# Sliding-window attention beside a gated layer: logits, softmax and weights of two chunks in one group each

## The chip, the cores and the metric

The kernel runs on one core of one Trainium2 chip. The metric is the device time of one execution in microseconds (us); the kernel before takes 259.79 us, the median of three runs (259.69 to 259.99). The engines that matter: TensorE (PE in the profile, PEld for its weight loads), VectorE (DVE), ScalarE (ACT), GpSimd (POOL) and SyncE (SP), which here issues most transfers.

## The reference

One input x (`A_x`, 2048 tokens by 640 features) goes through a layer norm. The normed x feeds two branches, an attention over a short dilated window and a gated layer, and both are added to x. The input `B_x` is not used.

```python
def _A_ref(x, wqkv, wo):            # 32 heads of 20, window W = 8, dilation 2
    qkv = ((x @ wqkv).reshape(B, S, 3, H, Dh)).transpose(2, 0, 3, 1, 4)
    q, k, v = qkv[0], qkv[1], qkv[2]
    idx = pos[:, None] - off[None, :]          # pos - 0, 2, 4, ... 14
    kg, vg = k at idx, v at idx                # (B, H, S, W, Dh)
    logits = einsum("bhsd,bhswd->bhsw", q, kg) * Dh ** -0.5
    logits = where(idx >= 0, logits, -1e9)
    o = einsum("bhsw,bhswd->bhsd", softmax(logits), vg)
    return o.transpose(0, 2, 1, 3).reshape(B, S, D) @ wo

def _B_ref(x, w_gate, w_up, w_down):           # 640 -> 1536 -> 640
    return ((x @ w_gate) * (x @ w_up)) @ w_down

xn = layernorm(A_x)
out = A_x + _A_ref(xn, A_wqkv, A_wo) + _B_ref(xn, B_w_gate, B_w_up, B_w_down)
```

## The kernel before

The 2048 tokens are four chunks (`NCH`) of 512 (`CS`), each four token tiles of 128 (`CH` = 4, `P` = 128). Features lie on the 128 partitions, 640 of them in five slices (`KT`). Head h owns four partitions (`JL`) of every slice, so a sum over a head's features is a sum over five slices and four partitions.

The stages of a chunk c:

- **Projections** (`proj`, L487 to L505): q, k and v, each five groups of five matmuls of 512 columns into PSUM tiles `ps` (six banks in turn), copied to SBUF by ScalarE (L498).
- **Products** (`products`, L543 to L563): for each half chunk of 256 tokens (`HS`), eight offsets in four VectorE multiplications q times shifted k into two tiles `pw` (L557), then **folds** (`fold`, L522): three additions each that sum the five slices; the last (L533) writes into the places of k and q that are no longer needed.
- **Logits** (`logits`, L569): matmuls with `Ek`, a matrix of 128 by 32 that sums each head's four partitions. Tokens of a half chunk are cut in four parts of 64 (`E` = HS // 4), and part j goes to the array's column strip j and thus to partitions 32j to 32j+31. So a group n = 2c + g is a PSUM tile `lps` of 128 partitions (part and head) by 8 offsets by 64 tokens: 512 floats, one PSUM bank, tag `pl` with two buffers. It is eight matmuls of 256 columns (L579), two groups per chunk.
- **Softmax** (`softmax`, L595): per group, on that tile in place: maximum over the offsets (L607), subtraction (L611), Exp on ScalarE (L620), sum (L627), reciprocal (L630), product into `a` (L634). Group 0 adds the mask first (L603).
- **Weights**: `store` (L640) writes `a` to a DRAM scratch tile `aD`, 128 KB, and `spread` (L646) reads it back into `aE` with each head's weights repeated on its four partitions, 512 KB, two buffers. Both are issued by SP.
- **Values** (`av`, L661): per token tile two multiplications of v by `aE`, one for each part of 64 tokens, 2560 elements each (L674); three additions that sum the eight offsets (L684 twice, L682) end in `oT`.
- **Gated layer** (`glu`, L708): twelve times five matmuls each for gate and up (L717), copies by ScalarE (L722), their product `hT` on VectorE (L734).
- **Output** (`down`, L769): per token tile and half of the 640 outputs, twelve matmuls from `hT` (L783) and five from `oT` (L786) add up in one PSUM bank; ScalarE copies them out (L798), and GpSimd adds them to the output in DRAM. For the first tile of a chunk the matmuls of `hT` 10 and 11 come last. The last two tiles go through VectorE (L794).

Nothing is written in the order in which it runs. Each step is registered by `add` with an engine, a planned cost, the part of it that occupies the engine (`occ`), and its dependencies; `Plan.order` then lists them. At each turn it takes the engine that is free first and, among its steps that are ready, the one that must be done first (`late`, counted back from the end); on TensorE all steps but the logits are a fixed chain (`main`), and logits are `urgent`: they go in as soon as the plan has them ready. `margin` adds time after a step's inputs before the plan takes it to be ready: 0.9 us for logits of chunk 0 and 2 for the others. `PACE` multiplies all planned times of an engine: 1.03 for VectorE. Engines then run their own lists in that order, and a step that isn't ready holds up what stands behind it.

```python
    PACE = {"DVE": 1.03, "ACT": 1.0}
```
```python
        LL[n].margin = (0.9 if c == 0 else 2) if alone else 0.0
```

The names in dependencies: `PW` products, `FO` folds, `LL` logits, `AA` the finished weights in SBUF, `AS` the store, `AE` the spread, `AM` a tile's last multiplication, `O16` and `OE` its oT, `HT` hT, `DT` a tile's last matmul. A spread waits for `AM.get(2 * n - 3)`, the last tile of the group two before. The first multiplication of a tile follows `AM.get(t - 1)`, since `ONE` is False.

The main loop at the end takes attention, gated layer, layer norm of chunk c + 2, output and the projections of chunk c + 2 for each c; the projections of chunks 0 and 1 come ahead.

Of the kernel before, what the change touches and what calls it, by code (L numbers as in the profile page):

```python
# [10 lines left out]
ALU = mybir.AluOpType  # L11
# [21 lines left out]
class Plan:  # L33
# [1 line left out]

    LAG = 0.06
    RAW = 0.116
    PACE = {"DVE": 1.03, "ACT": 1.0}
    INORDER = ("DVE", "PE", "ACT")

    def __init__(self):
# [70 lines left out]
def kernel(  # L112
# [314 lines left out]
            X[t + 5] = add("POOL", 6.0, load_x(t + 5, nc.gpsimd), [a], occ=0.45, kb=160)  # L427

    LL = {}
    PV = {}  # L430
    R = {}
    PROJ = ("q", "k", "v")
# [2 lines left out]
    def halo(c, r):  # L435
        def fn():
            k = new((PROJ[r], c), [P, KT, HALO + CS], BF, PROJ[r], 2)
            if c == 0:
                nc.gpsimd.memset(k[:, :, 0:HALO], 0.0)
            else:  # L440
                nc.scalar.copy(k[:, :, 0:HALO], T[PROJ[r], c - 1][:, :, CS : CS + HALO])
        if c == 0:
            HALOCP[r, c] = add("POOL", 0.3, fn, after=[RS[0]])
        else:
            w = LL.get(2 * c - 3) if r == 1 else O16.get(CH * (c - 1) - 1)
            HALOCP[r, c] = add("ACT", 0.25, fn, [w, *R[r, c - 1]])

    def lhs(r, i, j):
# [38 lines left out]
    def proj(c, r, lo=0, n=CS):  # L487
        for j in range(KT):
            key = ("qkv", c, r, j, lo)

            def pe(key=key, j=j):
                new(key, [P, 512], F32, "ps", 6, psum)
                for i in range(KT):
                    nc.tensor.matmul(T[key][:, 0:n], lhsT=lhs(r, i, j),  # L494
                                     rhs=T["xnT", c][:, i, lo : lo + n], start=(i == 0), stop=(i == KT - 1))

            def ev(key=key, j=j):
                nc.scalar.copy(where(r, c, j, j + 1, lo, n)[:, 0, :], T[key][:, 0:n])  # L498

            ts = range(c * CH + lo // P, c * CH + (lo + n) // P)  # L500
            old = LL.get(2 * c - 3) if r < 2 else O16.get(CH * (c - 1) - 1)
            a = pe_main(KT * (n / 2400 + 0.0027), pe, [*WW[r], *[TT[t] for t in ts], *[TX.get(t) for t in ts], old])
            e = add("ACT", 0.16 + n / 1200, ev, [a, HALOCP.get((r, c)), R.get((r, c - 2), [None])[0]], occ=0.07 + n / 1200)
            ring.append(e)
            R.setdefault((r, c), []).append(e)  # L505
# [37 lines left out]
    def products(c, hf):  # L543
        for j in range(4):
            i = 4 * hf + j
            u = i // 2

            def mul(u=u, j=j):
                if j % 2 == 0:
                    new(("pw", c, u), [P, 4, KT, HS], BF, *(("av", 2) if c == 0 and hf else ("pw", 2)))  # L550
                o = T["pw", c, u][:, 2 * (j % 2) : 2 * (j % 2) + 2, :, :]
                lo = hf * HS
                qh = T["q", c][:, :, lo : lo + HS]
                kh = T["k", c][:, :, lo + DIL * 2 * j : lo + DIL * 2 * j + HS]
                qh = bass.AP(tensor=qh.tensor, offset=qh.offset, ap=[list(qh.ap[0]), [0, 2], *[list(x) for x in qh.ap[1:]]])
                kh = bass.AP(tensor=kh.tensor, offset=kh.offset, ap=[list(kh.ap[0]), [DIL, 2], *[list(x) for x in kh.ap[1:]]])
                nc.vector.tensor_tensor(o, qh, kh, ALU.mult)  # L557

            m = 8 * c + i
            w = None if c == 0 else LL[0] if c == 1 and hf == 0 and FIRST < 3 else FO[4 * c + u - 2]  # L560
            PW[m] = add("DVE", 1.48, mul, [*R[0, c], *R[1, c], w], occ=1.395, after=[PW.get(m - 1)])
        for u in (2 * hf, 2 * hf + 1):
            FO[4 * c + u] = fold(c, u)  # L563

    PAIRED = ()

    E = HS // 4

    def logits(c, g):  # L569
        n = 2 * c + g  # L570

        def lg():
            l = new(("lps", n), [P, W, E], F32, "pl", 2, psum)
            parts = [summed(c, 2 * g + b) for b in range(2)]
            last = len(parts[0]) - 1
            for i in range(last + 1):
                for b in range(2):
                    for j in range(4):
                        nc.tensor.matmul(l[H * j : H * (j + 1), 4 * b : 4 * b + 4, :], lhsT=Ek[:],  # L579
                                         rhs=parts[b][i][:, :, E * j : E * (j + 1)],  # L580
                                         start=(i == 0 and b == 0), stop=(i == last), tile_position=(0, H * j), skip_group_check=True)

        alone = not (g and c in PAIRED)
        took = 0.022 + 0.2195 * (len(LEFT) if c == 0 else 1) + (0.19 if alone else 0.0)
        LL[n] = add("PE", took + 0.13, lg, [FO[2 * n], FO[2 * n + 1], FO[4 * c + 3] if c in PAIRED else None, LL.get(n - 1), AA.get(n - 2), CE], occ=took)
        LL[n].urgent = True
        LL[n].margin = (0.9 if c == 0 else 2) if alone else 0.0

    def prodlog(c):
        for g in range(2):  # L590
            products(c, g)
        for g in range(2):
            logits(c, g)

    def softmax(c, hf):  # L595
        n = 2 * c + hf

        def small(op, occ, deps):
            return add("DVE", occ + 0.083, op, deps, occ=occ)

        def mask():
            ps = T["lps", n]
            nc.vector.tensor_tensor(ps[0:H, :, 0:HALO], ps[0:H, :, 0:HALO], negm[0:H], ALU.add)  # L603

        def top():
            m = new(("m", n), [P, E], F32, "m", 1)
            nc.vector.tensor_reduce(m[:], T["lps", n][:].rearrange("p w s -> p s w"), AX.X, ALU.max)  # L607

        def sub():
            d = T["d", n] = T["lps", n]  # L610
            nc.vector.tensor_tensor(d[:], d[:], T["m", n][:, None, :].to_broadcast([P, W, E]), ALU.subtract)  # L611

        a = LL[n]
        if n == 0:
            a = small(mask, 0.18, [a, CM])
        a = small(top, 0.6, [a])
        DD[n] = small(sub, 0.609, [a, AA.get(n - 1)])

        def ex():
            nc.scalar.activation(T["d", n][:], T["d", n][:], ACT.Exp, scale=scale)  # L620

        e = add("ACT", 0.635, ex, [DD[n]], occ=0.54)
        e.margin = 0.8

        def total():
            s = new(("s", n), [P, E], F32, "s", 1)
            nc.vector.tensor_reduce(s[:], T["d", n][:].rearrange("p w s -> p s w"), AX.X, ALU.add)  # L627

        def rec():
            nc.vector.reciprocal(T["s", n][:], T["s", n][:])  # L630

        def scaled():
            a = new(("a", n), [P, W, E], BF, "a", 1)
            nc.vector.tensor_tensor(a[:], T["d", n][:], T["s", n][:, None, :].to_broadcast([P, W, E]), ALU.mult)  # L634

        AA[n] = small(scaled, 0.609, [small(rec, 0.47, [small(total, 0.6, [e])]), AS.get(n - 1)])

        def store():
            aD = new(("aD", n), [H, 4, W * E], BF, "aD", 2, dram)
            nc.sync.dma_start(out=aD[:].rearrange("h e f -> e h f"), in_=T["a", n][:].rearrange("p w s -> p (w s)"))  # L640

        def spread():
            ae = new(("aE", n), [P, 4, W, E], BF, "aE", 2)
            src = T["aD", n][:]
            src = bass.AP(tensor=src.tensor, offset=src.offset, ap=[[4 * W * E, H], [0, JL], [1, 4 * W * E]])
            nc.sync.dma_start(out=ae[:], in_=src)  # L646

        AS[n] = add("SP", 3.3, store, [AA[n], AE.get(n - 2)], occ=0.5, kb=128)
        AE[n] = add("SP", 3.9, spread, [AS[n], AM.get(2 * n - 3)], occ=0.5, kb=512)

    BY_DMA = ()
    AS = {}
    ONE = False

    def load_down():
        WL["d"] = SPLAST[0] = add("SP", 8, wload(wd, B_w_down), after=[SPLAST[0]], occ=0.5, kb=1920)
# [2 lines left out]
        WL["o"] = SPLAST[0] = add("SP", 8, wo_load, after=[SPLAST[0]], occ=0.5, kb=800)  # L659

    def av(t):  # L661
        n, u = divmod(t, 2)
        c, q = divmod(t, CH)

        def mul(b):
            def fn():
                if b == 0:
                    new(("av", t), [P, W, KT, P], BF, "av", 2)
                o = T["av", t][:, :, :, b * E : (b + 1) * E]
                w = T["aE", n][:, 2 * u + b, :, :]  # L670
                w = bass.AP(tensor=w.tensor, offset=w.offset, ap=[list(w.ap[0]), [E, W], [0, KT], [1, E]])
                v = T["v", c][:, :, q * P + b * E : q * P + b * E + E]
                v = bass.AP(tensor=v.tensor, offset=v.offset, ap=[list(v.ap[0]), [DIL, W], *[list(x) for x in v.ap[1:]]])
# [10 lines left out]
                    nc.vector.tensor_tensor(v[:, 0:k], v[:, 0:k], v[:, k : 2 * k], ALU.add)  # L684
            return fn

        w = LL[1] if t < 2 else O16.get(t - 2)
        a = add("DVE", 1.48, mul(0), [AE[n], w, *R[2, c]], occ=1.40, after=[O16.get(t - 1) if ONE else AM.get(t - 1)])
        a = AM[t] = add("DVE", 1.48, mul(1), [AE[n]], occ=1.40, after=[a])
        def tree_dma(k):  # L690
            def fn():
                v = T["av", t]
# [193 lines left out]
    def attention(c):  # L886
        prodlog(c)
        if c == 0:
            SPLAST[0] = WL["u"]
            load_down()  # L890
            load_out()
        for hf in range(2):
            softmax(c, hf)
        for q in range(CH):
            av(c * CH + q)

# [58 lines left out]
```

## Time and profile before

| what | value |
|---|---|
| median of three runs | 259.79 us (259.69 to 259.99) |
| the profiled execution | 258.83 us |
| its span, first to last instruction | 256.9 us |
| mean granted TensorE clock | 0.999 |
| ScalarE, GpSimd busy | 129.1 us (50%), 33.9 us (13%) |
| L579 matmuls | 64, 0.28 us each (256 columns) |
| L674 multiplications | 32, 47.6 us in all |
| VectorE's wait for aE | 8.9 us in 3 waits, longest 5.3 |

A line of a group of instructions has the line of the program, engine, operation, output and inputs, count, then busy time and the mean of one. In an answer in order of time each row starts with start and length in us. A chain of waits goes back from the last instruction, at each step to what released it or to the instruction before it on its engine: what lies on it sets the end. The time of the runs is longer than the span by what lies around it.

### The profile page before, as it was taken

The numbers are of one execution on the slowest core, as the hardware profiler recorded it, in microseconds if no ns is written. First come the engines' busy times: TensorE is split into PE (matmuls) and PEld (weight loads), VectorE is DVE, ScalarE is ACT, GpSimd is POOL, SyncE is SP. The second block draws the span as 40 slices with busy tenths as digits, with TensorE's granted clock in tenths as the row PEclk, the third lists the DMA queues.
The fourth block names the chain that finished last, engine by engine and source line by source line (L and its number), as shares of the span: only waits on it lengthen the run. The fifth ranks groups of instructions, "written<-read, shape, count | busy, mean of one in ns | idle before, by whom it ended". The sixth has DMA issues, their size and how long they took to land.

```text
span 256.9 us, 3821 instructions
## 1 busy us (share of the span) xinstructions
PE 251.4 (98%) x1493; PEld 140.3 (55%) x1493; DVE 226.2 (88%) x299; ACT 129.1 (50%) x251; POOL 33.9 (13%) x59
## 2 busy tenths in 40 slices
PE   6999999999999999999999999999999999999995
PEld 2955554444677555444477655444457654445762
DVE  5679999999999998999999964999999975999911
ACT  2756555798551364689662254655531233754100
POOL 2530000002142100003702110000301210000110
PEclk9999999999999999999999999999999999999999
DMA  7989996102165402032327232020022243020221
GB/s 224 346 200 239 397 374 225 69 23 82 25 117 95 46 12 93 0 102 102 106 52 98 32 46 82 7 97 0 27 79 26 26 61 94 20 82 3 26 26 52
DMA packets 19969, 24.48 MB, mean 95 GB/s; under 512 B 9104, under 2 KB 17296, under 8 KB 19888
## 3 DMA queue, kind: packets, MB, share of 16 engines
q1 hardware_dynamic: 16608, 17.70, 22.2%
q0 software_dynamic: 2384, 5.41, 12.4%
q10 hardware_dynamic: 960, 1.15, 1.3%
q8 instruction: 11, 0.18, 0.3%
q14 instruction: 6, 0.05, 0.1%
HBM read 18.61 MB, written 5.96 MB: 96 GB/s over the span
## 4 chain that ended last, share of the span: by engine, by line
PE 96%; DVE 1%; DMA 1%; ACT 0%; issue 0%
PE ps L717 40%; PE ps L494 23%; PE ps L783 20%; PE ps L786 8%; PE ps L468 2%; PE pl L579 1%; DMA x<-in_A_x_dram 1%; DVE st L252 1%; PE ps L393 0%; ACT xnT L399 0%; DVE x L271 0%; DVE x L794 0%; DVE mv L258 0%; DVE ve L260 0%
## 5 line engine op out<-in xcount | busy, mean ns | idle before, releaser
L717 PE MATMUL ps<-xnT,wu 128*128 128x512 bf16 x240 | 59.7, 379 | 0.0
L717 PE MATMUL ps<-xnT,wg 128*128 128x512 bf16 x240 | 59.6, 379 | 0.0
L783 PE MATMUL ps<-wd,hT 128*128 128x320 bf16 (+2 forms) x384 | 57.4, 299 | 0.0
L674 DVE TENSOR_TENSOR av<-v,aE 128x2560 bf16<-128x2560 bf16 x32 | 47.6, 1486 | 8.9 <-DMA aE<-aD 8.9
L783 PEld LDWEIGHTS <-hT 128*128 128x128 bf16 x384 | 37.0, 98 | 16.1 <-issue 0.4
L557 DVE TENSOR_TENSOR pw<-q,k 128x2560 bf16<-128x2560 bf16 x28 | 40.6, 1486 | 0.9 <-ACT k L498 0.9
L717 PEld LDWEIGHTS <-wg 128*128 128x128 bf16 x240 | 23.5, 98 | 28.1
L717 PEld LDWEIGHTS <-wu 128*128 128x128 bf16 x240 | 23.3, 98 | 28.3 <-issue 0.4
L684 DVE TENSOR_TENSOR av<-av 128x2560 bf16<-128x2560 bf16 (+1 forms) x32 | 36.9, 1154 | 0.3
L722 ACT CAST us<-ps 128x512 bf16<-128x512 f32 x48 | 28.2, 587 | 17.3 <-PE ps L717 17.3
L722 ACT CAST gs<-ps 128x512 bf16<-128x512 f32 x48 | 28.1, 586 | 16.7 <-PE ps L717 16.7
L798 ACT COPY y<-ps 128x320 f32<-128x320 f32 x28 | 11.7, 426 | 45.5 <-PE ps L786 30.7
L786 PE MATMUL ps<-wo,oT 128*128 128x320 bf16 (+2 forms) x160 | 27.0, 299 | 0.0
L528 DVE TENSOR_TENSOR pw<-pw 128x2048 bf16<-128x2048 bf16 (+1 forms) x28 | 25.2, 952 | 0.0
L827 POOL DMA_DIRECT2D out_dram<-y x14 | 12.3, 876 | 82.1 <-ACT y L798 81.6
L494 PE MATMUL ps<-xnT,wk 128*128 128x512 bf16 x100 | 22.6, 380 | 0.0
L734 DVE TENSOR_TENSOR hT<-gs,us 128x512 bf16<-128x512 bf16 x48 | 20.2, 420 | 2.6 <-ACT us L722 2.4
L494 PE MATMUL ps<-xnT,wv 128*128 128x512 bf16 x100 | 22.4, 379 | 0.0
L786 PEld LDWEIGHTS <-oT 128*128 128x128 bf16 x160 | 15.5, 98 | 6.3
L498 ACT CAST k<-ps 128x512 bf16<-128x512 f32 x20 | 11.7, 586 | 11.0 <-PE ps L494 11.0
L494 PEld LDWEIGHTS <-wv 128*128 128x128 bf16 x100 | 11.7, 118 | 9.9 <-issue 0.2
L494 PE MATMUL ps<-xnT,wq 128*128 128x512 bf16 x75 | 16.9, 379 | 0.0
(69 smaller groups left out, 197.0 us busy)
## 6 DMA issues: line engine op xcount, KB each, us to landing
aE<-aD SPq DMA_DIRECT2D x8, 512.0 KB, 3.6
out_dram<-y POOLq DMA_DIRECT2D x14, 160.0 KB, 3.6
out_dram<-in_A_x_dram POOLq DMA_DIRECT2D x3, 640.0 KB, 4.3
wg<-in_B_w_gate_dram SPq DMA_DIRECT2D x1, 1920.0 KB
wu<-in_B_w_up_dram SPq DMA_DIRECT2D x1, 1920.0 KB, 12.7
wd<-in_B_w_down_dram SPq DMA_DIRECT2D x1, 1920.0 KB
x<-in_A_x_dram SPq DMA_DIRECT2D x11, 160.0 KB, 6.4
aD<-a SPq DMA_DIRECT2D x8, 128.0 KB
```

The source lines that it names most:

```text
L494: nc.tensor.matmul(T[key][:, 0:n], lhsT=lhs(r, i, j), rhs=T["xnT", c][:, i, lo : lo + n], start=(i == 0), stop=(i == KT - 1))
L498: nc.scalar.copy(where(r, c, j, j + 1, lo, n)[:, 0, :], T[key][:, 0:n])
L528: nc.vector.tensor_tensor(w[:, :, lo:hi, :], w[:, :, lo:hi, :], w[:, :, a:b, :], ALU.add)
L557: nc.vector.tensor_tensor(o, qh, kh, ALU.mult)
L674: nc.vector.tensor_tensor(o, v, w, ALU.mult)
L684: nc.vector.tensor_tensor(v[:, 0:k], v[:, 0:k], v[:, k : 2 * k], ALU.add)
L717: nc.tensor.matmul(ps[:], lhsT=(wu if r else wg)[:, i, f * P : (f + 1) * P], rhs=T["xnT", c][:, i, :], start=(i == 0), stop=(i == KT - 1))
L722: nc.scalar.copy(s[:], T[key][:])
L734: nc.vector.tensor_tensor(h[:], T["gs", c, f][:], T["us", c, f][:], ALU.mult)
L783: nc.tensor.matmul(ps, lhsT=T["hT", c, f][:, q * P : (q + 1) * P], rhs=wd[:, f, sl], start=(f == 0), stop=(f == FT - 1 and not wo_part))
L786: nc.tensor.matmul(ps, lhsT=T["oT", t][:, g, :], rhs=wo[:, g, sl], start=False, stop=(g == KT - 1 and f1 == FT))
L827: nc.gpsimd.dma_start(out=out_flat[t * P : (t + 1) * P, :], in_=T["y", t][:], accum_op=ALU.add)
```

## The change

`GR = (2, 1, 1, 2)` says into how many groups each chunk's logits, softmax and weights are cut. Chunks 0 and 3 keep two of 64 tokens per part; chunks 1 and 2 become one group each with `E` = CS // 4 // GR[c] = 128. The steps are now named by (c, g).

- Logits: one PSUM tile per chunk of 1024 floats over two banks, one buffer in place of two of one bank. With one group the eight matmuls have 512 columns, each four offsets of 128 tokens, one bank for each four offsets. The group waits for all four folds, and for the last softmax of the chunk before.
- Softmax: the same five VectorE steps and Exp on 1024 elements for chunks 1 and 2. Tiles `m`, `s` and `a` are one per chunk.
- Weights: `store` and `spread` of 256 KB and 1 MB for chunks 1 and 2; `aE` is one tile per chunk with one buffer, and a spread waits for the last multiplication of the chunk before. They are planned at 3.6 and 4.2 us without `kb`, the plan's account of a queue's bytes.
- Values: one multiplication of 5120 elements per tile in chunks 1 and 2. `ONE` becomes True: a tile's first multiplication follows the oT of the tile before.
- Plan: `PACE` of VectorE 1.01; margin of logits outside chunk 0 1.5.

The diff, cut to its core:

```diff
-    PACE = {"DVE": 1.03, "ACT": 1.0}
+    PACE = {"DVE": 1.01, "ACT": 1.0}
...
+    GR = (2, 1, 1, 2)
...
-            w = LL.get(2 * c - 3) if r == 1 else O16.get(CH * (c - 1) - 1)
+            w = LL.get((c - 2, GR[c - 2] - 1)) if r == 1 else O16.get(CH * (c - 1) - 1)
...
     def logits(c, g):
-        n = 2 * c + g
+        n = (c, g)
+        E = CS // 4 // GR[c]
...
-            l = new(("lps", n), [P, W, E], F32, "pl", 2, psum)
-            parts = [summed(c, 2 * g + b) for b in range(2)]
...
+            if g == 0:
+                new(("lps", c), [P, 2 * CS], F32, "pl", 1, psum)
+            l = T["lps", c][:, g * W * E : (g + 1) * W * E].rearrange("p (w s) -> p w s", w=W)
...
                     for j in range(4):
-                        nc.tensor.matmul(l[H * j : H * (j + 1), 4 * b : 4 * b + 4, :], lhsT=Ek[:],
-                                         rhs=parts[b][i][:, :, E * j : E * (j + 1)],
...
+                        at = g * 4 * E + j * E
+                        rhs = summed(c, 2 * (at // HS) + b)[i][:, :, at % HS : at % HS + E]
+                        first = i == 0 and (b == 0 or GR[c] == 1)
+                        nc.tensor.matmul(l[H * j : H * (j + 1), 4 * b : 4 * b + 4, :], lhsT=Ek[:], rhs=rhs, start=first,
+                                         stop=(i == steps - 1), tile_position=(0, H * j), skip_group_check=True)
...
-        LL[n] = add("PE", took + 0.13, lg, [FO[2 * n], FO[2 * n + 1], FO[4 * c + 3] if c in PAIRED else None, LL.get(n - 1), AA.get(n - 2), CE], occ=took)
+        folds = [FO[4 * c + u] for u in range(4) if GR[c] == 1 or u // 2 == g]
+        LL[n] = add("PE", took + 0.13, lg, [*folds, LL.get(before.get(n)), AA.get((c - 1, GR[c - 1] - 1)), CE], occ=took)
         LL[n].urgent = True
-        LL[n].margin = (0.9 if c == 0 else 2) if alone else 0.0
+        LL[n].margin = 0.9 if c == 0 else 1.5
...
+            if g == 0:
+                new(("m", c), [P, P], F32, "m", 1)
+            nc.vector.tensor_reduce(mine("m", E), mine("lps", W * E).rearrange("p w s -> p s w"), AX.X, ALU.max)
...
-            ae = new(("aE", n), [P, 4, W, E], BF, "aE", 2)
+            if g == 0:
+                new(("aE", c), [P, 4 * W * P], BF, "aE", 1)
...
-        AS[n] = add("SP", 3.3, store, [AA[n], AE.get(n - 2)], occ=0.5, kb=128)
-        AE[n] = add("SP", 3.9, spread, [AS[n], AM.get(2 * n - 3)], occ=0.5, kb=512)
+        AS[n] = add("SP", 3.6, store, [AA[n], AE.get((c - 2, GR[c - 2] - 1))], occ=0.5)
+        AE[n] = add("SP", 4.2, spread, [AS[n], AM.get(CH * c - 1)], occ=0.5)
...
-    ONE = False
+    ONE = True
...
-        a = add("DVE", 1.48, mul(0), [AE[n], w, *R[2, c]], occ=1.40, after=[O16.get(t - 1) if ONE else AM.get(t - 1)])
-        a = AM[t] = add("DVE", 1.48, mul(1), [AE[n]], occ=1.40, after=[a])
+        ae = AE[c, q * GR[c] // CH]
+        a = None
+        for b in range(parts):
+            w = 0.065 + 2.67 / parts
+            a = add("DVE", w + 0.085, mul(b), [ae, LL[0, GR[0] - 1] if t < 2 else O16.get(t - 2), *R[2, c]], occ=w,
+                    after=[a or (O16.get(t - 1) if ONE else AM.get(t - 1))])
+        AM[t] = a
```

Here `mine(name, size)` is group g's part of the chunk's tile, `before` gives the group ahead, and `parts` is P // E, the multiplications of a tile.

## The prediction

> **What bounds the kernel now.** I read the page first: how long each engine is busy, and the chain that ended last.
>
> ```profile
> span 256.9 us, 3821 instructions
> PE 251.4 (98%) x1493; PEld 140.3 (55%) x1493; DVE 226.2 (88%) x299; ACT 129.1 (50%) x251; POOL 33.9 (13%) x59
> PE 96%; DVE 1%; DMA 1%; ACT 0%; issue 0%
> ```
>
> TensorE is the path from start to end: 96% of the chain. VectorE (DVE) is full to 88%, but a shorter VectorE shortens nothing by itself. So the change can gain only in TensorE's own instructions, and it loses wherever TensorE has to wait for a later VectorE. The second view is the chain in order of time, around three of the eight groups of logits matmuls (L579). Columns: start, length, instruction and count.
>
> ```profile
> 40.74 5.40 PE ps L717 x25
> 46.14 0.33 PE pl L579 x8
> 46.47 20.61 PE ps L717 x95
> ...
> 142.42 0.33 PE pl L579 x8
> 142.75 1.74 PE ps L783 x12
> 144.49 0.68 PE ps L786 x5
> 145.17 1.63 PE ps L783 x12
> ...
> 212.17 0.33 PE pl L579 x8
> ```
>
> There is no gap in it: TensorE never waits for logits, nor for anything else after the start. And a group costs more than its 0.33: the piece behind it is longer than its like. Twelve matmuls of L783 take 1.74 behind a group and 1.63 elsewhere (+0.11); the 95 of L717 take 20.61, where 95 x 5.40/25 = 20.52 (+0.09); behind the groups at 88.04, 156.44 and 31.98 the same subtraction gives 0.13. I take 0.12, so a group costs 0.45 us.
>
> The third view is VectorE in order of time, at the places where TensorE's next work hangs on it. Columns: start, length, line, operation; in brackets the idle time before and its releaser.
>
> ```profile
> 96.86 0.68 DVE L533 TENSOR_TENSOR q<-pw 128x1024 bf16<-128x1024 bf16 x1
> 101.03 1.49 DVE L674 TENSOR_TENSOR av<-v,aE 128x2560 bf16<-128x2560 bf16 x1 [0.68 <-DMA aE<-aD]
> 125.56 0.48 DVE L682 TENSOR_TENSOR oT<-av 128x640 bf16<-128x640 bf16 x1
> 130.41 0.49 DVE L682 TENSOR_TENSOR oT<-av 128x640 bf16<-128x640 bf16 x1
> 157.48 1.49 DVE L674 TENSOR_TENSOR av<-v,aE 128x2560 bf16<-128x2560 bf16 x1 [5.28 <-DMA aE<-aD]
> 209.81 0.69 DVE L533 TENSOR_TENSOR q<-pw 128x1024 bf16<-128x1024 bf16 x1
> 238.75 0.42 DVE L734 TENSOR_TENSOR hT<-gs,us 128x512 bf16<-128x512 bf16 x1
> ```
>
> From this and the chain I read reserves. Values: chunk 1's oT tiles end at 113.1, 119.6, 126.0, 130.9, and TensorE takes them at 129.9, 134.8, 139.4, 144.5, so 13 to 17 us in hand; chunk 2 has 20 to 24, chunk 3 has 7 to 10. Logits: chunk 1's last fold ends at 97.54 and its group starts at 101.12 (3.6 in hand); chunk 3's ends at 210.50, its group at 212.17 (1.7). The last hT of chunk 3 ends at 239.17; the piece that reads it starts at 239.35, so 0.2 in hand, the thinnest place of the kernel.
>
> The transfers between are in the same view of SP's queue, here of chunk 1's first half (start, time to issue):
>
> ```profile
> 94.03 0.54 SPq L640 DMA_DIRECT2D aD<-a  x1
> 97.32 0.55 SPq L646 DMA_DIRECT2D aE<-aD  x1
> ```
>
> **Part by part.** *Logits on TensorE (on the path).* Chunks 1 and 2 go from two groups of 8 matmuls with 256 columns to one group of 8 with 512; chunks 0 and 3 keep theirs. A 512-column matmul takes 5.40/25 = 0.216, so 256 columns stream in 0.108, and eight in a row would need 0.86. They need 0.33, so the four 32-column strips of the array run side by side: two rounds are 0.216, and 0.45 - 0.216 = 0.234 is fixed. One large group: 2 x 0.216 + 0.234 = 0.67, against 2 x 0.45 = 0.90. That saves 0.23 per chunk, 0.47 in all. Bounds: if nothing were fixed, the large group would cost 0.90 and save 0. If the 0.33 were the issue of eight instructions (0.041 each), the new group would take its stream, 0.432, plus 0.12, thus 0.55, and save 0.35 per chunk, 0.70 in all. I take 0.47: a 512-column stream is what the rows show directly, and something fixed is there, because the 0.12 is.
>
> The Trainium skill, "TensorEngine Tiling (Array Packing)", section "Performance Considerations", gives an overhead of about 60 cycles per matmul; as an estimate, with the 2.4 GHz of the Trainium skill's "Trainium Kernel Development and Optimization", section "NeuronCore Architecture", that is 25 ns, under the 41 ns of the row. By it issue is not the limit of the small group, and the saving would be the 0.47; by the row read as an issue rate it would be 0.70. No run here shows yet which.
>
> *Softmax on VectorE (off the path).* Rows of 512 float elements take 0.69 (L607, L611, L627, L634) and the reciprocal of 64 takes 0.55. L794 has 0.69 for 512 and 0.29 for 128 elements: 1.05 ns each, 0.15 fixed. So 1024 elements take 1.22, the reciprocal about 1.07, and Exp on ScalarE 0.59 + 512 x 0.84 = 1.02 (0.84 ns from 0.587 for 512 and 0.426 for 320). With about 0.04 between dependent steps, one pass is 1.26+1.24+1.07+1.26+1.10+1.23 = 7.2. Two halves held VectorE for 2 x 3.25 (88.14 to 89.47 and 92.00 to 93.92); one whole holds it for 6.0, so 0.5 less per chunk.
>
> *Value multiplication.* 2560 elements take 1.486, 1280 take 0.822 (L684), so 5120 take 1.486 + 1.328 = 2.81, issued 2.73 apart, against 2 x 1.40: 0.07 for each of eight tiles, 0.6 in all. ONE = True holds the next tile's first multiplication behind oT; then up to 0.12 opens between dependent steps (two tree steps: 2.34 where 2.22 are work), 16 x 0.12 = 1.9 at most, partly filled by hT products. VectorE so ends between 1.6 lighter and 0.3 heavier. Its idle time (257 - 226) covers that; without this cover it would add what it overruns.
>
> *Later values (moved).* The first values of a chunk now wait for all four folds. In chunk 1 work up to the last fold ran from 76.46 to 97.46; without the 3.25 of softmax inside it ends at 94.2. Logits follow some 3.1 later (3.6 as now, 0.5 less margin) and end at 98.0; softmax ends at 105.2. Store and spread took 7.0 (store issued at 94.03, values start at 101.03) and carry twice the bytes: 7.0 if only the fixed part counts, 14.0 if all doubles. POOL's transfers of 160 KB land in 3.6 and those of 640 KB in 4.3, so the extra 640 KB are nearer the low end; I take 8 to 10. Values then start at 114 (119 at worst) instead of 101. A tile is 2.73+1.40+0.74+0.41+0.1, with three hT products of 0.34 between: 6.4. The oT tiles end at 120.4, 126.8, 133.2, 139 (at worst 5 later: 144) against 129.9 to 144.5. What this hides behind is the 13 to 17 us in hand; 4 to 9 stay, at worst 0.5. In chunk 2, with over 20, more stays. While the transfer runs, VectorE has products and folds of the next chunk to do (q and k of chunk 2 are there by 97.46, where L557 already ran ahead), so its work is rearranged, not lengthened. Queued on SP behind the spread is nothing that is due: the next are the four transposes at 130.18, and for chunk 2 the store at 206.98. In VectorE's queue hT products stand behind a late multiplication; gs and us have 5 and 4 buffers at one per 2.16, so some 8 us. The single aE buffer makes chunk 3's first spread wait for chunk 2's last multiplication, which ended at 182.0 and will end some 12 later; the spread was issued at 210.31.
>
> *Planner's reserves.* PACE falls from 1.03 to 1.01: the 1.40 of a multiplication was planned as 1.44, now 1.41. Since VectorE's work from 157.48 to 210.50 runs without a long wait, the plan is 53 x 0.02/1.03 = 1.0 earlier there; the logits margin gives up another 0.5. Chunk 3's second group keeps 1.7 - 1.5 = 0.2. No stall, so I cost it at nothing, but anything later by more than 0.2 lands on TensorE one for one, since its matmuls follow one another as written. Bounds: 0 to +1.5 (the whole reserve).
>
> **Sum.** TensorE -0.47, the rest 0. The profiled execution took 258.83 (span 256.9 and 1.93 around it), so 258.36; the median of the runs is 259.79, so **259.32**.
>
> **Rivals.** *Small group is issue-bound:* saving 0.70, 259.09. For it: eight matmuls at an even 41 ns; against: the fixed 0.12 belongs to something else than issue. *No fixed part:* 0, 259.79; against it speaks that 0.12. *Reserve spent:* one or two waits of TensorE, at a logits group or the last hT of a chunk, of 0.3 to 1.5 in sum, centre 0.8: 260.12. For it: the 0.2 in hand at two places, and an order that is made anew; against: not one such wait now. *Exposed transfer (the slower side):* VectorE doesn't fill the softmax and transfer time of chunks 1 and 2. Each would leave it idle for some 10 us; of 20 us, the idle of 5.28 and 2.96 that is there now, 1.6 of lighter work and chunk 3's 6.6 in hand come off, and 3.6 are left; 261.3 at half of that and 263 at the whole. The place is the oT tiles of chunk 3, and it decides from about 16 us of new idle. For it: VectorE already waits 5.28 there when q and k of chunk 3 aren't ready; against: products of chunk 2 ran ahead at 97.46. The Trainium skill, "Trainium Kernel Development and Optimization", section "Best Practices", tells to double-buffer so that transfers overlap compute; aE and the logits' PSUM tile become single, which by that rule speaks for this rival.
>
> **Chances.** Forecast 0.41, issue-bound 0.13, no fixed part 0.06, reserve spent 0.24, exposed transfer 0.16. A difference under 0.2% (0.52 us, bounds 259.27 and 260.31) can't be told from none here. Faster: 0.4 of the forecast (it lies 0.05 from the bound) and nine tenths of issue-bound: 0.28. Slower: 0.4 of reserve spent and all of exposed transfer: 0.26. Within: 0.46. The forecast's own range is 259.1 to 259.6; that for all cases, 258.9 to 261.2, leaves out the worse half of exposed transfer and the tails, about 0.1.
>
> **What would show it.** Right: six logits groups in the chain, two of them with the following piece's excess at 0.67; no wait of TensorE after the start; oT of chunk 1 between 120 and 140; multiplications of 2.81. Wrong: the chain running through VectorE or a transfer before a group, an hT or an oT; a large group at 0.55 or 0.90; VectorE idle for over 16 us more.

## The result and the profile after

The changed kernel is slower: 261.41 us (median of 22 runs, 260.00 to 263.91) against 259.76 (22 runs of the kernel before, 259.17 to 260.29), a ratio of 1.0063 with a 95% interval of 1.0049 to 1.0078. The forecast was 259.32, the range 258.9 to 261.2. Its runs also lie further apart, 3.9 us where the kernel before has 1.1.

The profiled execution took 263.61 us and lies near the top of that spread. From its page, the span and the chain that ended last by engine:

```profile
span 261.9 us, 3740 instructions
PE 69%; DVE 19%; DMA 9%; issue 1%; ACT 1%; SPq 0%
```

Before, TensorE was 96% of the chain; now VectorE and transfers stand in it. TensorE in order of time shows where (start, length; in brackets the idle time before and its releaser). From 7 us on these are the only pieces with a wait that the view lists:

```profile
133.51 2.55 PE L813 MATMUL ps<-wd,hT 128*128 128x320 bf16 x16 [0.85 <-DVE hT L764]
...
197.82 3.89 PE L813 MATMUL ps<-wd,hT 128*128 128x320 bf16 x15 [2.57 <-DVE hT L764]
```

Both are the piece that reads hT 10 and 11 of a chunk, 1 and then 2: the last hT products (hT 11 alone in chunk 2) come late. VectorE, followed backwards from there, tells why:

```profile
117.48 2.83 DVE L698 TENSOR_TENSOR av<-v,aE 128x5120 bf16<-128x5120 bf16 x1 [3.33 <-DMA aE<-aD]
...
130.30 2.82 DVE L698 TENSOR_TENSOR av<-v,aE 128x5120 bf16<-128x5120 bf16 x1
133.03 0.75 DVE L764 TENSOR_TENSOR hT<-gs,us 128x512 bf16<-128x512 bf16 x2
...
175.39 2.83 DVE L698 TENSOR_TENSOR av<-v,aE 128x5120 bf16<-128x5120 bf16 x1 [4.22 <-DMA aE<-aD]
...
194.61 2.82 DVE L698 TENSOR_TENSOR av<-v,aE 128x5120 bf16<-128x5120 bf16 x1
197.35 0.42 DVE L764 TENSOR_TENSOR hT<-gs,us 128x512 bf16<-128x512 bf16 x1
```

At the first multiplication of each of the two chunks VectorE's list stands for 3.33 and 4.22 us until the weights have landed. From there to the last hT products it doesn't pause, and the third or fourth multiplication is written ahead of them: what was lost at 117 is still lost at 133. The transfers, in the view of SP's queue:

```profile
105.90 0.53 SPq L662 DMA_DIRECT2D aD<-a  x1
111.76 0.55 SPq L669 DMA_DIRECT2D aE<-aD  x1
...
162.66 0.55 SPq L662 DMA_DIRECT2D aD<-a  x1
168.55 0.55 SPq L669 DMA_DIRECT2D aE<-aD  x1
```

From the store's issue to the multiplication it is 11.6 us in chunk 1 and 12.7 in chunk 2. The plan that wrote the lists reckons 3.6 + 4.2 = 7.8. (In chunk 2 VectorE also stands 2.39 us for Exp, ahead of the store; runs 1 and 7 below have that wait too, and lose nothing by it.)

The second wait costs more than itself. TensorE by the microsecond, with its granted clock (stretch, length, busy and count, clock, share of the DMA engines, GB/s):

```profile
196.00:197.00 1.00, 0.00 (x0) 1.00 0.00 0
197.00:198.00 1.00, 0.18 (x1) 0.94 0.00 0
198.00:199.00 1.00, 1.00 (x5) 0.50 0.07 16
199.00:200.00 1.00, 1.00 (x6) 0.50 0.00 0
200.00:201.00 1.00, 1.00 (x6) 0.50 0.00 0
201.00:202.00 1.00, 1.00 (x8) 0.85 1.08 81
```

Behind the 2.57 us without work the clock is at half for about 3.4 us, and the 15 matmuls of L813 take 3.89 where the same 15 behind the first wait take 2.21: 1.7 more. In the chain that ended last (start, length):

```profile
133.84 2.21 PE ps L813 x15
...
197.82 3.89 PE ps L813 x15
...
258.91 0.29 PE ps L816 x5
```

The last of these is TensorE's last piece. In the first profile of the kernel before it is

```profile
253.47 0.29 PE ps L786 x5
```

so it starts 5.44 us later now. By the starts of like pieces in the two traces, the output of chunk 0 begins 0.27 later than before, the logits save 0.46 (below), 1.2 are lost around the first wait and 4.4 around the second. The span is only 5.0 longer, since what follows the last matmul is 0.5 shorter. Only this one of the 22 runs was traced. The clock is 1.0 in 20 of the other 21, and the span of these 258.0 to 260.5, so they lose less; that they lose it in the same way is not shown by a trace, but run 7 below removes the loss of the median too.

### The profile page after: what moved, and what is told of

It is laid out like the page before. It is cut to its first block, busy times and chain, and to the rows that moved or that the text cites. A ratio compares the mean times of both kernels' runs of the same rounds, so it can differ in the third digit from the quotient of the medians.

```text
span 261.9 us, 3740 instructions
## 1 busy us (share of the span) xinstructions
PE 253.1 (97%) x1458; PEld 141.1 (54%) x1477; DVE 226.0 (86%) x281; ACT 129.5 (49%) x249; POOL 30.9 (12%) x59
## 3 DMA queue, kind: packets, MB, share of 16 engines
q0 software_dynamic: 2384, 5.41, 12.7%
## 4 chain that ended last, share of the span: by engine, by line
PE 69%; DVE 19%; DMA 9%; issue 1%; ACT 1%; SPq 0%
PE ps L747 20%; PE ps L813 19%; PE ps L495 18%; DVE av L698 7%; PE ps L816 7%; DMA aE<-aD 5%; DMA aD<-a 4%; DVE av L708 4%; PE ps L469 2%; DVE hT L764 2%; PE ps L243 2%; DVE pw L558 1%; DVE a L653 1%; PE pl L586 1%; DVE s L644 1%
## 5 line engine op out<-in xcount | busy, mean ns | idle before, releaser
L813 PE MATMUL ps<-wd,hT 128*128 128x320 bf16 (+2 forms) x383 | 59.4, 305 | 3.5 <-DVE hT L764 3.4
L698 DVE TENSOR_TENSOR av<-v,aE 128x2560 bf16<-128x2560 bf16 (+1 forms) x24 | 46.2, 1930 | 7.6 <-DMA aE<-aD 7.6
L813 PEld LDWEIGHTS <-hT 128*128 128x128 bf16 x384 | 37.6, 100 | 21.1 <-DVE hT L764 4.3
L495 PE MATMUL ps<-xnT,wk 128*128 128x512 bf16 x97 | 22.3, 380 | 0.2
L495 PE MATMUL ps<-xnT,wv 128*128 128x512 bf16 x99 | 22.2, 379 | 0.1
L495 PEld LDWEIGHTS <-wv 128*128 128x128 bf16 x100 | 11.7, 118 | 10.1 <-issue 0.4
L495 PEld LDWEIGHTS <-wk 128*128 128x128 bf16 x100 | 11.5, 118 | 9.8 <-issue 0.5
L495 PE MATMUL ps<-xnT,wq 128*128 128x512 bf16 x72 | 16.5, 379 | 0.2
```

The source lines that it names most:

```text
L495: nc.tensor.matmul(T[key][:, 0:n], lhsT=lhs(r, i, j), rhs=T["xnT", c][:, i, lo : lo + n], start=(i == 0), stop=(i == KT - 1))
L698: nc.vector.tensor_tensor(o, v, w, ALU.mult)
L813: nc.tensor.matmul(ps, lhsT=T["hT", c, f][:, q * P : (q + 1) * P], rhs=wd[:, f, sl], start=(f == 0), stop=(f == FT - 1 and not wo_part))
```

## The experiments

Theory A is what the profile says: VectorE's list is written for weights that land 4 to 5 us before they do. Rival B: the planner's reserves, PACE and margin, were given up. Rival C: an undivided multiplication of 2.82 us holds hT up whenever it starts. Rival D, added later: the large group as such, late and long. The kernel before was run beside each; ratios are to it.

**1. The true costs.** No operation changes, only what the plan reckons, and by that the order.

```diff
-        AS[n] = add("SP", 3.6, store, ...
-        AE[n] = add("SP", 4.2, spread, ...
+        AS[n] = add("SP", 6.0 if GR[c] == 1 else 3.6, store, ...
+        AE[n] = add("SP", 6.6 if GR[c] == 1 else 4.2, spread, ...
```

> The changed kernel, with the large group's store planned at 6.0 us and its spread at 6.6 us instead of 3.6 and 4.2 (measured: 5.84 and 5.70 in chunk 1, 5.81 and 6.82 in chunk 2); the order is made anew, no operation changes. Theory A (the list of VectorE is written for weights that land 4 to 5 us before they do, so the last hT products stand behind late multiplications): the waits of TensorE for hT (0.85 and 2.57 us) fall under 0.3 us in sum, 259.3 to 259.7 us. Rival B (the reserve of PACE and margin was given up): the waits stay, 260.5 to 262 us. Rival C (a multiplication of 2.82 us holds hT up whenever it starts): 260.3 to 261 us.

Measured 258.19 us, ratio 0.9952 (0.9938 to 0.9966): faster than both kernels, and below what A expected. Its profile has no wait of TensorE after 7 us. The order is a new one, so this run alone could be a lucky list; run 7 keeps the list. Its chain shows what the large group costs:

```profile
96.82 0.54 PE pl L586 x8
97.36 5.52 PE ps L495 x25
...
152.66 0.55 PE pl L586 x8
153.20 10.92 PE ps L495 x50
```

25 matmuls of L495 are 5.40 elsewhere, 50 are 10.80: so 0.54 + 0.12 = 0.66 and 0.55 + 0.12 = 0.67.

**2. The reserves back.** PACE 1.03 and margin 2 in the changed kernel.

> The changed kernel with PACE of VectorE 1.03 and the margin of logits 2 us, as before. Theory A: the transfers are as late as in the changed kernel against the plan, waits for hT of 1 us or more stay, 260.3 to 262 us. Rival B: no waits, 259.2 to 259.6 us. Rival C: 260.3 to 261 us.

Measured 259.46, ratio 1.0001 (0.9991 to 1.0011): the time is in Rival B's range, and A's number was missed. The mechanism is between the two, since B expected no waits: the profile has one, 0.89 us for hT in chunk 1, and VectorE still stands 6.2 us for aE in two waits. Larger reserves, with the new order that they write, make a list that bears late weights better; they do not make the weights land sooner. So the reserves that were given up are a part of why late weights reached TensorE.

**3. Two groups everywhere.** `GR = (2, 2, 2, 2)`, all else as changed.

> The changed kernel with two groups in every chunk; PACE, margin, ONE, the single buffers and the planned costs 3.6 and 4.2 stay. Theory A: the planned 7.8 us meet transfers that took 7.0 us in this size, so no waits for hT; eight small groups of logits cost 0.4 us more than six: 259.6 to 260.0 us, and little spread between runs. Rival B: waits as in the changed kernel, 260.5 us or more. Rival C: 259.6 to 260.0 us.

Measured 259.13, ratio 0.9985 (0.9977 to 0.9994), runs within 0.7 us, no wait of TensorE after 7 us. Small reserves alone, with transfers that take the 7.0 us planned at 7.8, do no harm: B fails here as a cause by itself.

**4. The multiplication cut in two.**

```diff
-        parts = P // E
+        parts = 2
```
(with the slices of `aE`, v and `av` for half a tile)

> The changed kernel with each value multiplication of chunks 1 and 2 cut into two of 2560 elements, so that an hT product can go between; logits, softmax, weights and their transfers stay in one group. Theory A: the list is still some 4 us late when the last hT products come, 260.5 to 261.8 us. Rival C (the undivided 2.82 us): waits gone or under 0.4 us, 259.4 to 260.0 us. Rival B: 260.5 to 262 us.

Measured 260.08, ratio 1.0022 (1.0011 to 1.0032), waits of 1.20 us (chunk 1) and 0.31 (chunk 3). That is under A's range and above C's. In chunk 1, where VectorE still stands 3.27 us for aE, the wait is no shorter than with whole pieces (0.85); in chunk 2 none is left, but there VectorE stands only 1.93 us for aE. So the piece's length is not the source; whether it adds to the wait isn't shown, because the list is a new one.

**5. The kernel before, once more.**

> The kernel before, profiled once more. Its first profiled execution took 258.83 us and had no wait of TensorE after the start, but its median is 259.5 to 259.8 us. If the median holds waits that the first profile escaped (theory A as it bears on the kernel before: the last hT of chunk 3 had 0.2 us in hand, that of chunk 2 0.7), this profile at about 259.5 us shows 0.5 to 1 us of waits of TensorE for hT. Rival: no waits, and the time lies around the span or is spread over all matmuls.

Measured 259.57, span 257.7, and one wait of TensorE, in the same view as above:

```profile
240.08 2.21 PE L783 MATMUL ps<-wd,hT 128*128 128x320 bf16 x15 [0.58 <-DVE hT L734]
```

It is the last hT of chunk 3, where the first profile had 0.2 us in hand. That profile (258.83) had escaped what this one, nearer the median, has.

**6. Small groups, planned too short.** Run 3 with store and spread of chunks 1 and 2 planned at 1.4 and 1.9 us.

> Two groups in every chunk, as in the third run above, but the stores and spreads of chunks 1 and 2 are planned at 1.4 and 1.9 us, 3.7 us less than the 7.0 they take, as the changed kernel plans its large ones 3.8 to 4.9 us too short. No operation changes. Theory A: waits of TensorE for hT come back, 259.8 to 262 us. Rival D (it is the large group as such: its late start, its single long chain): no waits, 259.0 to 259.4 us.

Measured 273.22, ratio 1.0505 (1.0476 to 1.0535). The waits for hT are back (6.2 us in five), and there are more: the logits wait for folds (1.7 and 0.5 us), the gated layer for k (1.2), and the clock is at half for about 10 us. The direction is A's and D is refuted as a necessary cause; the size was far under-estimated.

**7. Faster transfers, same order.** The scratch tile is written part by part, the spread is four transfers; planned costs stay at 3.6 and 4.2.

```diff
-                new(("aD", c), [GR[c], H, 4, W * E], BF, f"aD{GR[c]}", 2, dram)
-            ... out=T["aD", c][g].rearrange("h e f -> e h f"), ...
+                new(("aD", c), [GR[c], 4, H, W * E], BF, f"aD{GR[c]}", 2, dram)
+            ... out=T["aD", c][g].rearrange("e h f -> (e h) f"), ...
-            src = bass.AP(..., ap=[[4 * W * E, H], [0, JL], [1, 4 * W * E]])
-            nc.sync.dma_start(out=T["aE", c][:, g * 4 * W * E : (g + 1) * 4 * W * E], in_=src)
+            for e in range(4):
+                part = bass.AP(..., offset=src.offset + e * H * W * E, ap=[[W * E, H], [0, JL], [1, W * E]])
+                nc.sync.dma_start(out=T["aE", c][:, (g * 4 + e) * W * E : (g * 4 + e + 1) * W * E], in_=part)
```

> The changed kernel with its planned costs (3.6 and 4.2), but faster transfers: the DRAM scratch tile is laid out part by part, so that the store writes it in one run of 128 rows, and the spread is four transfers, one for each part, the first of which is all that the first tile of a chunk needs. Theory A: store near 3.3 us, first part 3.5 us behind it, 7 us in all where 7.8 are planned, so no waits for hT: 258.1 to 258.6 us as with the true costs. Rival B: waits stay, 259.4 us or more. Rival D: waits stay, since the group starts as late and is as long: 260 us or more.

Measured 258.60, ratio 0.9947 (0.9930 to 0.9964). This is the cleanest of the runs: the lists of TensorE, VectorE, ScalarE and GpSimd are instruction by instruction those of the changed kernel, and only the transfers differ. SP's queue and VectorE in chunk 1:

```profile
106.05 0.33 SPq L662 DMA_DIRECT2D aD<-a  x1
108.14 2.46 SPq L670 DMA_DIRECT2D aE<-aD  x4
```

```profile
114.21 2.82 DVE L699 TENSOR_TENSOR av<-v,aE 128x5120 bf16<-128x5120 bf16 x1
...
129.76 0.75 DVE L765 TENSOR_TENSOR hT<-gs,us 128x512 bf16<-128x512 bf16 x2
```

The 3.33 us ahead of the multiplication are gone (114.21 against 117.48), the same two hT products start at 129.76 in place of 133.03, 3.27 earlier, and TensorE does not wait. The small reserves, the single buffers, `ONE` and the undivided multiplication are all still there, so none of them makes TensorE wait without the late weights.

**8. The kernel before with the new reserves.** PACE 1.01, margin 1.5, ONE = True; nothing else of the change.

> The kernel before with PACE 1.01, margin 1.5 and ONE = True, and nothing else of the change. Theory A: the planned 7.2 us are the real 7.0, so the smaller reserve costs nothing or little: 259.0 to 259.8 us. Rival B (the reserve): waits of 1 us or more, 260.3 us or more.

Measured 264.55, ratio 1.0181 (1.0149 to 1.0214): B's side, it seemed. But the expectation had the plan wrong. With `kb` the plan takes a store to land after 2 + 128/340 and a spread after 2 + 512/340, 5.9 us in all, not 7.2; 7.0 are measured. So this too was a list written for weights that come early, and the kernel before has lived with the same error.

**9. The same without `kb`.** Store and spread of run 8 planned at 3.6 and 4.2.

> The run before this (the kernel before with PACE 1.01, margin 1.5 and ONE = True, 264.55 us) with one thing more from the change: store and spread planned at 3.6 and 4.2 us without kb. With kb the plan reckons a store to land after 2 + 128/340 = 2.4 us and a spread after 2 + 512/340 = 3.5 us, so 5.9 us, where 7.0 are measured; now it reckons 7.8. No operation changes. Theory A (weights planned to land before they do): the waits for hT vanish, 259.0 to 259.6 us. Rival B (PACE and margin): 262 us or more, as without it.

Measured 258.98, ratio 0.9974 (0.9963 to 0.9986), no wait for hT. Of 264.55 us, 5.6 went with two numbers of the plan; the reserves stayed as small. The lists of the four engines come out as those of run 3, so 259.13 and 258.98 are one result found in two ways, and not two.

**10. The kernel before without `kb`.** Only that.

> The kernel before with nothing but store and spread planned at 3.6 and 4.2 us without kb (7.8 instead of the 5.9 us that its plan reckons). Theory A: the wait of 0.6 us for chunk 3's last hT that the median of the kernel before holds goes, 258.9 to 259.3 us. Rival: as before, 259.4 to 259.9 us.

Measured 259.20, ratio 0.9986 (0.9974 to 0.9998), and no wait of TensorE for hT. VectorE's last hT of chunk 3 and the piece that reads it:

```profile
236.67 0.42 DVE L734 TENSOR_TENSOR hT<-gs,us 128x512 bf16<-128x512 bf16 x1
```
```profile
239.22 2.34 PE L783 MATMUL ps<-wd,hT 128*128 128x320 bf16 x16
```

The product ends at 237.09, so 2.1 us are in hand where the kernel before had 0.2. The gain, 0.5 us, fits the wait of run 5. It is small against the noise, though, and the profiled execution (258.88) is among the fastest of its kernel, so that the other executions have no wait either isn't shown.

**11. True costs and the old reserves.** Run 1 with PACE 1.03 and margin 2.

> The changed kernel with the true costs of the large transfers (6.0 and 6.6, 258.19 us) and with PACE 1.03 and margin 2 as before. Theory A: nothing is left for the reserve to prevent, 258.1 to 258.5 us. Rival B: the reserve buys more, under 258.0 us.

Measured 261.20, ratio 1.0061 (1.0041 to 1.0081): outside both. TensorE waits in other places:

```profile
133.21 2.21 PE L813 MATMUL ps<-wd,hT 128*128 128x320 bf16 x15 [0.17 <-DVE hT L764]
145.77 0.85 PE L816 MATMUL ps<-wo,oT 128*128 128x320 bf16 x5 [0.86 <-DVE oT L706]
150.42 3.41 PE L495 MATMUL ps<-xnT,wq 128*128 128x512 bf16 x15 [1.49 <-DMA xnT<-x]
```

The last is a transpose of chunk 3's input, and the chain leads from it back over ScalarE's layer norm to GpSimd's queue, which stood at the gate L794 (8.66 us in the chain). A list made anew meets other errors of the plan; more reserve is no remedy in itself.

**12. Fast transfers and costs that match them** (store 2.4, spread 5.0).

> The changed kernel with the four spreads and the new scratch layout, and with plan costs that match them: store 2.4 us (2.1 measured in chunk 1), spread 5.0 us to its last part. Theory A: no waits of TensorE, 258.0 to 258.6 us, no better than the true costs with the slow transfers (258.19) or the fast ones with the old costs (258.60), since with no waits left only TensorE's own instructions count. Rival E (every new order is a draw; the earlier gains were luck): 259 us or more is as likely.

Measured 258.43, ratio 0.9962 (0.9946 to 0.9979), no wait of TensorE. But the lists of the four engines come out as in run 7 and in the changed kernel: no new order was written, so this is run 7 once more, and it can't speak against Rival E. What does is run 7 itself, where the list stayed and the loss went. Runs 1 and 7 agree within 0.4 us from two sides, plan and transfer. That the size of a new list's loss can't be foretold, as Rival E has it, run 11 shows.

## Why the prediction was wrong

**What bounds the kernel: right,** and it says why a late VectorE costs. The kernel could gain only TensorE's own instructions.

**Logits: right.** 0.67 was forecast for the large group, 0.66 and 0.67 measured (run 1); two small ones at 0.45 cost 0.90, so 0.46 is gained where 0.47 was forecast. From the first output of chunk 0 to the last piece TensorE needs 0.48 us less in run 1 (67.56 to 253.47) than in the first profile of the kernel before (67.08 to 253.47). Between runs 3 and 1, both without waits after 7 us, its last matmul ends 0.3 to 0.4 us earlier; their medians lie 0.94 apart, and the rest of that is not explained. Both other prices of the group (issue-bound, no fixed part) fall.

**Softmax and multiplications: right.** 1.22 for 1024 elements (1.22 to 1.24), 0.95 for the reciprocal (1.07 forecast), 2.82 for 5120 (2.81).

**Store and spread: mis-sized, and the first half of the error.** I took 8 to 10 us with bounds of 7 and 14; it was 11.6 and 12.7. I had read the price of more bytes from GpSimd's transfers. The store has a shape of its own: in its stretch the DMA engines are busy to about a quarter.

```profile
107.10:111.40 4.30, 4.25 (x21) 1.94 (x21) 4.25 (x6) 2.82 (x6) 0.00 (x0) 1.00 0.24 60
```

The columns are the stretch, its length, the busy time of TensorE, its weight loads, VectorE, ScalarE and GpSimd, the clock, the DMA share and GB/s: 0.24 of the 16 engines' time, 60 GB/s. With the scratch laid out so that the store writes 128 rows and not four parts of 32, the same 256 KB land in 2.0 us instead of 5.8 (median of run 7's issues below, columns: issue, count, size, us to landing). The Trainium skill, "DMA: Bandwidth & Descriptors", section "Why a DMA increments its semaphore by 16 and not by 1", has the number of engines of a transfer as the largest one up to 16 that divides the slowest dimension of both sides; with four parts as the slowest dimension of the target that is four of 16. The trace agrees: 0.24 is close to 4 of 16 (0.25).

```profile
aE<-aD SPq DMA_DIRECT2D x8, 256.0 KB, 3.5
...
aD<-a SPq DMA_DIRECT2D x2, 256.0 KB, 2.0
```

**Later values: the step that failed.** The forecast set the oT tiles against TensorE's need, and there it held: the first ended at 123.97 (120.4 forecast, 125.4 at worst), the last at 142.2, none late. Of the hT products it said only that gs and us have buffers for some 8 us, and the sum put a late multiplication ahead of them at nothing. That holds for those in the midst of a chunk. For the last two the reserve is what TensorE has to do between its last matmul of the gated layer and the piece that reads them, 1.36 + 0.68 + 1.36 + 0.68 = 4.1 us, less what the copy, the product itself and the multiplication ahead of it still take of that time. With weights on time hT 10 of chunk 1 ends at 130.18 (run 7, same list); TensorE wants it at 132.66 (133.51 less its wait): 2.5 us in hand. It ended at 133.45, 3.3 later, and 0.8 are the wait. My own 8 to 10 us beside the plan's 7.8 said that VectorE's list would stand still at the first multiplication; that stillness should have been carried on along the list to the next thing that TensorE takes from it, which is the last hT and not an oT.

**Planner's reserves: right that they were thin, wrong in the price.** The place named in "reserve spent", the last hT of a chunk, is where it went; its 0.3 to 1.5 us were 0.85 + 2.57 in the profiled execution, and "one for one" misses the halved clock, 1.7 more. Between the medians, 261.41 and the 258.60 of run 7, which has the same list, lie 2.8 us.

**The base.** The sum was made against an execution of 258.83 and shifted to the median by a constant. The 0.8 us between the spans was mostly no constant but the 0.58 us wait that this execution escaped (run 5). 258.36 was the sum against that execution, and 258.19 is what the kernel takes once it has no waits (run 1). That the two agree so well is in part luck: in run 1 the output of chunk 0 began 0.48 later than in that execution and what follows the last matmul was 0.46 shorter, neither of them in the forecast. Nor did it see that the change also mends the plan of chunks 0 and 3, which now reckons 7.8 us where it reckoned 5.9 and 7.0 are measured; that plan by itself was worth some 0.5 us in the kernel before (run 10).

**What stays open.** What the untraced runs of the changed kernel lose where, and why the sizes of runs 2, 6 and 11 came out so far from any forecast: each new set of costs writes a new list, and what a list costs was read only afterwards.

## What to carry to other kernels

Where a planner writes in-order lists, a planned duration that is too short can cost far more than the error: what stands behind the waiting instruction is late by the whole wait until the list has a pause, and the engine that pays may be another one, at another product. After changing a transfer's size or shape, measure issue to use and put that number into the plan before judging the change. Look at the engine share of a slow transfer: here a quarter of the engines went with its layout.

## What the runs showed of the hardware

TensorE's clock fell to half behind waits of 2.57 us (changed kernel) and 2.24 us (run 8), for about 3.4 us each time, and not behind 1.58 us (run 6, 15 matmuls in 2.21 as usual). In another place of run 6 it fell at 199.2, when two waits of 0.58 and 1.43 us with one matmul between them had just passed and a third, of 2.30, began, and it stayed at half for about 10 us. Each of the two is shorter than the 1.58 that did nothing, so waits close together count as well as a long one. The Trainium skill, "TensorE: Matmul & The Clock Gate", section "What's actually happening", has the slow state follow an idle window of some 3.4 us; here less was enough, while the 3.4 us of its length agree in the changed kernel and run 8, and not in run 6. Eight matmuls in four 32-column strips took 0.33 us at 256 columns and 0.54 to 0.57 at 512, and both times the next piece was 0.09 to 0.13 longer.
